# Whole loads of k, four small loads on another queue, two new ordering waits and one new rule of a planner

## The chip, the cores and the metric

The kernel runs on one NeuronCore of a Trainium2 chip. The metric is the device time of one execution in microseconds (us). Engines are named as the profile names them: PE (matmul) with PEld (its weight loads), DVE (VectorE), ACT (ScalarE), POOL (GpSimd), SP (SyncE, which here only issues DMAs). "SPq" and "ACTq" are DMA issues on SP and on ACT.

## The reference

Batch 4, 12 heads, 448 tokens, head size 64, so a model width of 768.

```python
def _attn_ref(q, k, v, g_q, g_k):
    q_n, k_n = (rmsnorm(q, g_q), rmsnorm(k, g_k))
    scores = scale * np.matmul(q_n, k_n.transpose(0, 1, 3, 2))
    scores = scores - np.max(scores, axis=-1, keepdims=True)
    attn = np.exp(scores)
    attn = attn / (np.sum(attn, axis=-1, keepdims=True) + 1e-09)
    return np.matmul(attn, v)
...
# then, per token or over tokens:
h = np.maximum(x @ w_in, 0.0); u, v = split(h)             # gated mixer
gated = u * (w_spatial over tokens of layernorm(v) + b);  x = gated @ w_out
u = x + (relu(x.T @ w_tok1) @ w_tok2).T                    # second mixer
out = u + relu(u @ w_ch1) @ w_ch2
```

g_q and g_k are vectors of 64 numbers, which reach the scores as one product.

## The kernel before

The 48 heads are worked in 24 pairs. For a pair, q and k (each 112 partitions x 4 chunks x 2 heads x 64) are loaded into one tile `raw`. ACT squares both halves into `sq` (for the very first k into a tile named `e`), DVE sums the squares into `ss`, POOL and ACT make the inverse root (`r0a`, `r0y`, `r0z` for q and `r8a`, `r8y`, `r8z` for k of the first pair; `ra`, `ry`, `rz` later), `raw` is scaled in place (DVE for the first pair, POOL later), PE transposes it into a PSUM tile `tp`, and a copy with the product `gg` of g_q and g_k gives k its gains. In the first 8 pairs the two transposed tiles are named `whole`, later `qt` and `kt`. PE then makes the scores `sc`, for one chunk of 112 tokens of both heads at a time: each head has 64 rows, so a score matmul fills half of the array's rows, and the two heads run beside each other. DVE takes the negated row maximum `nm`, ACT the exponential `e` with its sum. PE transposes `e` (`tp<-ident,e`), ACT or DVE copies it to `et`, and PE makes `av` from `et` and v: 64 output columns a head, half of the array's columns, again two heads beside each other. v lies in `v32` and its last 64 tokens in `vrest`, which holds zeros in its other half.

After six pairs (one batch entry) the first mixer's matmuls (`vps`, `ups`, `sps`, `xps`) are ready to run among the attention work of later pairs; the second mixer (`h1ps`, `u_ps`, `h2ps`, `o_ps`) follows. The weights arrive as 64-bit floats: `raw` pieces of them are turned into 32-bit numbers by ACT and DVE in tiles named `word` (for w_in's second half) and `wpart`.

Nothing of this is written in issue order by hand. `Plan` records every operation with an assumed cost, and `place` is a list scheduler, run forwards and backwards over the recorded operations, whose result is the order of each engine; all instructions are therefore issued at one line (L422). On PE `place` keeps half-array work together: when the next operation is of another kind than the one before (`parts` 1 for scores, 2 for `av`, 0 for the whole array) it looks for a waiting operation of the kind in hand that is nearly as urgent (`NEAR`). Each engine runs its instructions strictly in the order it was given. DMA completions are counted on 8 semaphores in rotation (named DMAHW0 to DMAHW7 in the order's rows), shared by SP's and ACT's DMAs: a ninth DMA waits until the one eight places earlier has landed.

The program opens (`start`) with 26 matmuls on zeros (`warm`), while the first two pairs are loaded.

Of the kernel before, what the change touches and what calls it, by code (L numbers as in the profile page):

```python
# [21 lines left out]
HI, LO = 0, 1  # L22
# [127 lines left out]
class Plan:  # L150
# [116 lines left out]
    def place(self, before, after, lag, weight, tiles=None):  # L267

        ops = self.ops
        left = [len(x) for x in before]  # L270
        ready = [0.0] * len(ops)
        engines = sorted({op.engine for op in ops})
        due = {e: [] for e in engines}
        waiting = {e: [] for e in engines}
        free_at = dict.fromkeys(engines, 0.0)
        start = [0.0] * len(ops)
        parts, port = 0, 0.0
        bank = {}
        if tiles is not None:
            opens, closes, users = tiles  # L280
            users = dict(users)
            free_banks = [(0.0, n) for n in range(Banks.ALL)]
            held = dict.fromkeys(Banks.OWN, 0)
            blocked = []
        for i, op in enumerate(ops):
            if not left[i]:
                heapq.heappush(due[op.engine], (0.0, i))
        placed = 0
        while placed < len(ops):
            t, e = min(  # L290
                (free_at[e] if waiting[e] else max(free_at[e], due[e][0][0]), e)
                for e in engines if waiting[e] or due[e])
            free_at[e] = t
            while due[e] and due[e][0][0] <= t:
                i = heapq.heappop(due[e])[1]
                heapq.heappush(waiting[e], (weight[i], i))
            i = heapq.heappop(waiting[e])[1]
            if e == "tensor" and ops[i].parts != parts:

                near = [x for x in waiting[e] if ops[x[1]].parts == parts and x[0] <= weight[i] + NEAR]  # L300
                if near:
                    x = min(near)
                    waiting[e].remove(x)
                    waiting[e].append((weight[i], i))
                    heapq.heapify(waiting[e])
                    i = x[1]
            other = SHARED.get(e)
            if ops[i].port and port <= t and other in due and free_at[other] <= t:

                free_at[other] = t  # L310
                while due[other] and due[other][0][0] <= t:
                    x = heapq.heappop(due[other])[1]
                    heapq.heappush(waiting[other], (weight[x], x))
                if waiting[other] and waiting[other][0][0] < weight[i] and ops[waiting[other][0][1]].port:
                    heapq.heappush(waiting[e], (weight[i], i))
                    e = other
                    i = heapq.heappop(waiting[e])[1]
            if ops[i].port:
                if port > t:
                    heapq.heappush(due[e], (port, i))  # L320
                    continue
                port = t + ops[i].cost
            if tiles is not None and i in opens:
                ks = opens[i]
                kind = ks[0].psum
                spare = len(free_banks) - sum(max(0, n - held[x]) for x, n in Banks.OWN.items() if x != kind)
                if spare < len(ks):
                    blocked.append(i)
                    continue
                free_banks.sort()  # L330
                at = free_banks[len(ks) - 1][0]
                if at > t:
                    heapq.heappush(due[e], (at, i))
                    continue
                for k in ks:
                    n = max(x for x in free_banks if x[0] <= t)
                    free_banks.remove(n)
                    bank[k] = n[1]
                held[kind] += len(ks)
            placed += 1  # L340
            start[i] = t
            end = t + ops[i].cost
            if e == "tensor":
                end += SWITCH * (ops[i].parts != parts)
                parts = ops[i].parts
            free_at[e] = end
            for s, hop in zip(after[i], lag[i]):
                ready[s] = max(ready[s], end + hop)
                left[s] -= 1
                if not left[s]:  # L350
                    heapq.heappush(due[ops[s].engine], (ready[s], s))
            if tiles is not None:
                for k in closes.get(i, ()):
                    users[k] -= 1
                    if not users[k]:
                        at = end + ops[i].late + TO["tensor"]
                        free_banks.append((at, bank[k]))
                        held[k.psum] -= 1
                        for x in blocked:
                            heapq.heappush(due["tensor"], (at, x))  # L360
                        blocked = []
        return start, max(free_at.values()), bank
# [107 lines left out]
def attention_moe_mixer(  # L470
# [7 lines left out]
    nc = tc.nc  # L478
# [55 lines left out]
    def wdram(w):  # L534
        return w.bitcast(U32)

    def convert(pool, tag, bufs, raw, rows, n, dst_hi, dst_lo, dims=None, at=None):

        if f64:
            r = raw.rearrange("p (n w) -> p n w", w=2)  # L540
            a = pool.tile([rows, n], U32, tag=tag, bufs=bufs, name="word") if at is None else at
            low, high = r[:, :, 0], r[:, :, 1]
            nc.scalar.activation(a.bitcast(F32), high.bitcast(F32), AF.Abs)
            nc.vector.tensor_scalar(a.bitcast(F32), a.bitcast(F32), least, most, ALU.max, ALU.min)
            nc.vector.tensor_scalar(a, a, 5, 2, ALU.logical_shift_left, ALU.logical_shift_right)
            nc.vector.scalar_tensor_tensor(a, high, 0xC0000000, a, ALU.bitwise_and, ALU.bitwise_or)
            nc.vector.scalar_tensor_tensor(a, low, 29, a, ALU.logical_shift_right, ALU.bitwise_or)
        else:
            a = raw
        a = a.bitcast(F32)  # L550
        if dst_hi is not None:
            v = a.rearrange("p (a b) -> p a b", a=dims[0]) if dims else a
            nc.scalar.activation(dst_hi, v, AF.Copy)
            nc.gpsimd.tensor_tensor(dst_lo, v, dst_hi.bitcast(F32), op=ALU.subtract)
        return a
# [43 lines left out]
    def mm_tile(name):  # L599
        return psum.tile([P, 512], "mm", name)  # L600

    def rsqrt(pool, src, n, w, mul, tag, bufs=2, on=None):

        on = on or nc.vector
# [3 lines left out]
        on.tensor_scalar(a[:n], src, mul, 1e-6, ALU.mult, ALU.add)  # L608
        nc.scalar.activation(y[:n], a[:n], AF.Ln)
        nc.scalar.activation(y[:n], y[:n], AF.Exp, scale=-0.5)  # L610
        on.tensor_tensor(z[:n], y[:n], y[:n], op=ALU.mult)
        on.tensor_tensor(z[:n], z[:n], a[:n], op=ALU.mult)
        on.tensor_scalar(z[:n], z[:n], -0.5, 1.5, ALU.mult, ALU.add)
# [7 lines left out]
    class Attention:  # L621
# [9 lines left out]
        def load(self, i):  # L631
# [4 lines left out]
            for r in range(2):  # L636
                nc.sync.dma_start(
                    out=t[:, 0, :, r], in_=q[b, 2 * j + r].rearrange("(c p) d -> p c d", p=T))
            on = nc.sync if i else nc.scalar
            on.dma_start(out=t[:, 1, :, 0], in_=k[b, 2 * j].rearrange("(c p) d -> p c d", p=T))  # L640

            src = k[b, 2 * j + 1]
            on.dma_start(out=t[:R, 1, 0, 1], in_=src[LAST:])
            on.dma_start(out=t[R:, 1, 0, 1], in_=src[:T - R])
            on.dma_start(
                out=t[:, 1, 1:, 1], in_=src[T - R:LAST].rearrange("(c p) d -> p c d", p=T))
            self.raw[i] = t
            if i == 2:
                self.third = t.tile
# [1 line left out]
        def load_v(self, i):  # L651
# [4 lines left out]
            rest = self.rests[i % VB]  # L656
            for r in range(2):
                src = v[b, 2 * j + r]
                nc.sync.dma_start(out=t[:, r], in_=src[:LAST].rearrange("(c p) d -> p c d", p=P))
                nc.sync.dma_start(out=rest[r * R:(r + 1) * R, r], in_=src[LAST:])  # L660
            self.v32[i] = t, rest

        def norms(self, i):
# [6 lines left out]
            for h in (slice(0, n // 2), slice(n // 2, n)):  # L670
# [2 lines left out]
                    sq = sq[:, :n // 2 * D].rearrange("p (n d) -> p n d", d=D)  # L673
                else:
                    sq = p.tile([T, n // 2, D], F32, tag="sq", bufs=1, name="sq")
                nc.scalar.activation(sq, raw[:, h], AF.Square)
                nc.vector.reduce_sum(ss[:T, h], sq, axis=AX.X)
                if i == 0:
# [155 lines left out]
        def start(self):  # L834
            self.load(0)
            g = self.p.tile([P, 2], F32, tag="g", bufs=1, name="g")
            for r in range(2):
                nc.sync.dma_start(out=g[r * D:(r + 1) * D, 0:1], in_=g_q.unsqueeze(1))
                nc.sync.dma_start(out=g[r * D:(r + 1) * D, 1:2], in_=g_k.unsqueeze(1))
            self.gg = self.p.tile([P, 1], F32, tag="gg", bufs=1, name="gg")  # L840
            nc.vector.tensor_tensor(self.gg, g[:, 0:1], g[:, 1:2], op=ALU.mult)
            nc.vector.tensor_scalar(self.gg, self.gg, float(D) ** -0.5, None, ALU.mult)
# [48 lines left out]
    ET, EB = 2 * C - 1, 5  # L891
    ON_DVE = (1, 1), (3, 1)
    SLOT = 8
    WARM = 26
    TWO = 99
    PREP0, LAG, SPAN = 1, 0.2, 5.8
    UO0, UO1 = 3, 11.5
# [4 lines left out]
    def prepare_v(mp):  # L902
# [5 lines left out]
        for j in range(KD):  # L908

            wait = [op for _, op in at.third.writers] if j > 1 else ()  # L910
            raw = weights(mp, "vn", 4, wdram(w_in)[j * P:(j + 1) * P, DU * W:], P, (DU,), wait)
            convert(mp, "vr", 2, raw, P, DU, wv[:, HI, j], wv[:, LO, j])
            yield
        for c in range(C):
            s = mp.tile([T, S], F32, tag="vn", bufs=4, name="stage")
# [570 lines left out]
```

## Time and profile before

| | |
|---|---|
| median of 3 runs | 891.25 us (890.48 to 892.96) |
| the profiled execution: its time | 892.5 us |
| its span (first to last instruction) | 890.7 us, 1.8 us less than its time |
| PE busy | 867.3 us, 97% of the span |
| DVE, ACT, POOL busy | 684.7, 538.3, 416.7 us |
| granted PE clock, mean | 0.996 of full speed |

A busy time is a sum over the whole span and over stages with different limits. The clock is given as a share of 2.4 GHz; 0.50 is 1.2 GHz.

### The profile page before, as it was taken

To read this page: it belongs to the slowest core of one execution; us is meant where nothing else is said; L and a number is where in the kernel's file an instruction comes from. 1 tells how busy PE (TensorE), PEld (TensorE's weight loads), DVE (VectorE), ACT (ScalarE), POOL (GpSimd) and SP (SyncE) were. 2 spreads that over 40 slices of the span, in tenths; PEclk is the share of its full clock that TensorE was granted. 3 is DMA by queue.
4 is the path that set the end of the run, shared out by engine and by line. 5 is a ranking of instruction groups with operands and counts; after the bars stand their busy time and mean duration, and the time that the engine had idled before them with its cause. 6 is when DMAs were issued, how large, how long until landed. Compare 5 with 4: busy or idle time off the path is not lost.

```text
span 890.7 us, 15921 instructions
## 1 busy us (share of the span) xinstructions
PE 867.3 (97%) x5186; PEld 721.6 (81%) x5186; DVE 684.7 (77%) x1333; ACT 538.3 (60%) x1292; POOL 416.7 (47%) x541
## 2 busy tenths in 40 slices
PE   7898999999999999999999999999999999999998
PEld 5444567787777787777789999999988899999998
DVE  4799897877877867976565466889888886998973
ACT  4999988777876777776543446546324554343331
POOL 3555654795676745665233214234323207524550
PEclk8999999999999999999999999999999999999999
DMA  6555645757535565335687559677564745661441
GB/s 152 154 133 156 193 126 162 203 175 229 162 105 159 151 203 160 90 123 166 211 267 250 178 179 319 194 242 231 157 160 133 230 125 155 213 182 54 142 151 63
DMA packets 149106, 152.30 MB, mean 171 GB/s; under 512 B 77856, under 2 KB 130656, under 8 KB 147488
## 3 DMA queue, kind: packets, MB, share of 16 engines
q1 hardware_dynamic: 148064, 151.06, 56.8%
q8 instruction: 41, 0.67, 0.3%
q14 instruction: 41, 0.34, 0.1%
q10 hardware_dynamic: 960, 0.23, 0.1%
HBM read 112.44 MB, written 38.80 MB: 170 GB/s over the span
## 4 chain that ended last, share of the span: by engine, by line
PE 77%; ACT 9%; DVE 8%; DMA 3%; issue 2%; SPq 0%; POOL 0%; ACTq 0%; DVEq 0%
PE o_ps L422 15%; PE h2ps L422 15%; PE tp L422 8%; PE xps L422 6%; PE ups L422 6%; PE av L422 6%; PE vps L422 5%; PE sc L422 5%; PE sps L422 4%; ACT e L422 4%; PE h1ps L422 3%; PE u_ps L422 3%; ACT et L422 2%; DVE op L422 1%; DVE w L422 1%
## 5 line engine op out<-in xcount | busy, mean ns | idle before, releaser
L422 PE MATMUL h2ps<-op,w 128*128 128x448 f32 x756 | 155.8, 367 | 2.4 <-DVE c L422 2.3
L422 PE MATMUL o_ps<-w,op 128*128 128x384 f32 x882 | 153.6, 334 | 1.2 <-DVE u L422 1.2
L422 PEld LDWEIGHTS o_ps<-w,op 128*128 128x128 f32 x882 | 152.8, 188 | 1.8 <-issue 1.8
L422 PEld LDWEIGHTS h2ps<-op,w 128*128 128x128 f32 x756 | 141.1, 188 | 15.7 <-DVE c L422 4.4
L422 ACT ACTIVATE e<-sc,nm 112x448 f32<-112x448 f32 x192 | 122.5, 653 | 25.3 <-DVE nm L422 25.1
L422 DVE TENSOR_REDUCE nm<-sc 112x1 f32<-112x448 f32 x192 | 109.5, 615 | 17.3 <-PE sc L422 17.0
L422 POOL TENSOR_TENSOR src<-src 128x384 f32<-128x384 f32 x48 | 62.7, 1314 | 77.6 <-DMA src<-c_d 40.6
L422 PEld LDWEIGHTS tp<-ident,e 112*128 112x128 f32 x672 | 71.8, 141 | 32.9 <-ACT et L422 9.3
L422 POOL TENSOR_SCALAR e<-e,sums 112x448 f32<-112x448 f32 x112 | 75.3, 690 | 40.9 <-ACT sq L422 9.7
L422 PE MATMUL tp<-ident,e 112*128 112x112 f32 x672 | 88.7, 262 | 4.6 <-ACT et L422 2.4
L422 ACT ACTIVATE op<-c 128x768 fp32r<-128x768 f32 x49 | 41.5, 847 | 84.6 <-PE o_ps L422 81.2
L422 ACT ACTIVATE et<-tp 128x448 f32<-128x448 f32 x144 | 71.3, 530 | 15.3 <-PE tp L422 14.4
L422 DVE SCALAR_TENSOR_TENSOR word<-raw,word 128x256 uint32<-128x256 uint32 (+2 forms) x132 | 72.2, 553 | 1.4
L422 POOL TENSOR_TENSOR u<-u,o 128x384 f32<-128x384 f32 x28 | 40.2, 1453 | 66.5 <-ACT o L422 35.8
L422 DVE TENSOR_SCALAR word<-word 128x256 f32<-128x256 f32 (+5 forms) x132 | 59.6, 458 | 15.0 <-ACT word L422 14.2
L422 PE MATMUL ups<-xp,wu 128*128 128x448 f32 x288 | 69.1, 376 | 0.0
L422 DVE TENSOR_TENSOR op<-c,op 128x768 fp32r<-128x768 f32 x49 | 57.4, 1172 | 10.3 <-ACT op L422 10.3
L422 PE MATMUL xps<-wo,g 128*128 128x256 f32 x432 | 60.5, 289 | 0.0
L422 PE MATMUL vps<-wv,xp 128*128 128x512 f32 x216 | 59.7, 409 | 0.0
L422 PE MATMUL av<-et,v 128*64 128x448 f32 x288 | 59.6, 548 | 0.0
L422 PEld LDWEIGHTS xps<-wo,g 128*128 128x128 f32 x432 | 54.7, 190 | 5.8 <-issue 2.3
L422 DVE TENSOR_TENSOR c<-c,h2ps 128x448 f32<-128x448 f32 x84 | 50.0, 616 | 11.0 <-PE h2ps L422 10.3
(141 smaller groups left out, 1661.9 us busy)
## 6 DMA issues: line engine op xcount, KB each, us to landing
src<-c_d SPq DMA_DIRECT2D x132, 192.0 KB, 3.1
wu<-wu_d SPq DMA_DIRECT2D x16, 768.0 KB, 4.8
wo<-wo_d SPq DMA_DIRECT2D x12, 1024.0 KB, 5.4
raw<-in_moe_w_ch_dram SPq DMA_DIRECT2D x36, 256.0 KB, 3.5
raw<-in_moe_w_ch_dram SPq DMA_DIRECT2D x24, 384.0 KB, 3.7
raw<-in_q_dram SPq DMA_DIRECT2D x48, 112.0 KB, 2.9
u<-u_d SPq DMA_DIRECT2D x28, 192.0 KB, 3.9
out_dram<-u SPq DMA_DIRECT2D x28, 192.0 KB, 2.0
```

Of the source, the lines that this page charges most:

```text
L422: getattr(getattr(self.nc, op.engine), fn)(*args, **kwargs)
```

## The change

Six edits, in one version:

- k of the second head of a pair is loaded in token order by one DMA, where it was rolled by 64 tokens and came in three. The roll is made up for by v: the second head's `vrest` now takes the first 64 tokens and not the last. A pair has 2 DMAs for k in place of 4, and the same bytes.
- The four DMAs of g_q and g_k are issued from ACT, not from SP.
- The first two `word` tiles of the weight w_in wait for the copy that writes the first pair's k (`wait=behind`).
- The first Square of pair 1 waits for the two Exp operations of pair 0's inverse roots (`powers[:2]`).
- Where PE's next operation is of the whole array and half-array work was in hand, `place` may now take waiting half-array work of either kind, not of the same kind alone.
- 18 matmuls on zeros, not 26.

```diff
@@ place
                 near = [x for x in waiting[e] if ops[x[1]].parts == parts and x[0] <= weight[i] + NEAR]
+                if not near and parts and not ops[i].parts:
+                    near = [x for x in waiting[e] if ops[x[1]].parts and x[0] <= weight[i] + NEAR]
...
@@ convert
+            a.tile.after = list(a.tile.after) + list(wait)
...
@@ load
-            on.dma_start(out=t[:, 1, :, 0], in_=k[b, 2 * j].rearrange("(c p) d -> p c d", p=T))
-
-            src = k[b, 2 * j + 1]
-            on.dma_start(out=t[:R, 1, 0, 1], in_=src[LAST:])
-            on.dma_start(out=t[R:, 1, 0, 1], in_=src[:T - R])
-            on.dma_start(
-                out=t[:, 1, 1:, 1], in_=src[T - R:LAST].rearrange("(c p) d -> p c d", p=T))
+            for r in range(2):
+                on.dma_start(
+                    out=t[:, 1, :, r], in_=k[b, 2 * j + r].rearrange("(c p) d -> p c d", p=T))
...
@@ load_v
-                nc.sync.dma_start(out=t[:, r], in_=src[:LAST].rearrange("(c p) d -> p c d", p=P))
-                nc.sync.dma_start(out=rest[r * R:(r + 1) * R, r], in_=src[LAST:])
+
+                most, least = (src[:LAST], src[LAST:]) if r == 0 else (src[R:], src[:R])
+                nc.sync.dma_start(out=t[:, r], in_=most.rearrange("(c p) d -> p c d", p=P))
+                nc.sync.dma_start(out=rest[r * R:(r + 1) * R, r], in_=least)
...
@@ norms
+                    if i == 1:
+
+                        sq.tile.after = list(sq.tile.after) + powers[:2]
...
@@ start
-                nc.sync.dma_start(out=g[r * D:(r + 1) * D, 0:1], in_=g_q.unsqueeze(1))
-                nc.sync.dma_start(out=g[r * D:(r + 1) * D, 1:2], in_=g_k.unsqueeze(1))
+                nc.scalar.dma_start(out=g[r * D:(r + 1) * D, 0:1], in_=g_q.unsqueeze(1))
+                nc.scalar.dma_start(out=g[r * D:(r + 1) * D, 1:2], in_=g_k.unsqueeze(1))
...
-    WARM = 26
+    WARM = 18
...
@@ prepare_v
-            convert(mp, "vr", 2, raw, P, DU, wv[:, HI, j], wv[:, LO, j])
+
+            behind = [] if wait else [op for _, op in at.kt[0].tile.writers]
+            convert(mp, "vr", 2, raw, P, DU, wv[:, HI, j], wv[:, LO, j], wait=behind)
```

The planner then makes new orders for all engines. At three places they are shown here.

The first place is ACT from its first DMA to its first exponential (`e,sums<-sc,nm`). What each instruction waits for stands in brackets; DMAHW is the semaphore of a DMA. Before:

```order
L422 DMA raw<-in_k_dram 48x64 [waits DMAHW0_49]
L422 ACTIVATE sq<-raw 112x512 [waits DMAHW1_49]
L422 ACTIVATE e<-raw 112x512 [waits DMAHW4_49,DMAHW6_49,DMAHW2_49,DMAHW0_49]
...
L422 ACTIVATE ry<-ra 112x16 [waits Pool_49]
L422 ACTIVATE word<-raw 128x512 [waits DMAHW0_49]
L422 ACTIVATE whole<-tp,gg 128x448 [waits DVE_49,PE_49]
L422 ACTIVATE ry<-ry 112x16 [waits Activation_49]
L422 ACTIVATE word<-raw 128x512 [waits DMAHW1_49]
L422 ACTIVATE e,sums<-sc,nm 112x448 [waits DVE_49] x4
```

And now:

```order
L424 DMA g<-in_g_q_dram 64x1 [waits DMAHW1_49]
L424 DMA g<-in_g_k_dram 64x1 [waits DMAHW3_49]
L424 ACTIVATE sq<-raw 112x512
L424 ACTIVATE e<-raw 112x512 [waits DMAHW4_49,DMAHW2_49]
...
L424 ACTIVATE whole<-tp,gg 128x448 [waits PE_49]
L424 ACTIVATE ry<-ra 112x16 [waits Pool_49]
L424 ACTIVATE word<-raw 128x512 [waits DMAHW4_49]
L424 ACTIVATE ry<-ry 112x16 [waits Activation_49]
L424 ACTIVATE word<-raw 128x512 [waits DMAHW5_49]
L424 ACTIVATE wpart<-raw 128x256 [waits DMAHW2_49]
L424 ACTIVATE e,sums<-sc,nm 112x448 [waits DVE_49] x4
```

The copy of the first k (`whole<-tp,gg`) moved ahead of both `word` conversions, and a `wpart` conversion moved ahead of the exponentials. The first Square (`sq`) now stands behind four DMA issues, the last of which waits for DMAHW3; that semaphore is held by pair 1's first q, the fourth DMA of the program.

The second place is DVE at the same time, up to the first maxima (`nm`). Before:

```order
L422 TENSOR_REDUCE ss<-sq 112x8 [waits Activation_49]
L422 TENSOR_TENSOR gg<-g 128x1 [waits DMAHW6_49,DMAHW7_49,DMAHW5_49,DMAHW4_49]
L422 TENSOR_REDUCE ss<-sq 112x8 [waits Activation_49]
L422 TENSOR_TENSOR raw<-raw,r0y 112x512 [waits DMAHW1_49,DMAHW0_49,Pool_49]
L422 TENSOR_TENSOR raw<-raw,r8y 112x512 [waits DMAHW2_49,DMAHW0_49,Pool_49]
```

And now:

```order
L424 TENSOR_TENSOR gg<-g 128x1 [waits DMAHW3_49,DMAHW6_49,DMAHW1_49,DMAHW0_49]
L424 TENSOR_SCALAR gg<-gg 128x1 [waits DVE_49]
L424 TENSOR_REDUCE ss<-sq 112x8 [waits Activation_49]
L424 TENSOR_TENSOR raw<-raw,r0y 112x512 [waits Pool_49]
L424 TENSOR_TENSOR raw<-raw,r8y 112x512 [waits DMAHW4_49,DMAHW2_49,Pool_49]
L424 TENSOR_REDUCE ss<-sq 112x8 [waits Activation_49]
```

One of the two sums for pair 1 (`ss<-sq`) moved behind the scaling of pair 0; the other still stands ahead of it.

The third place is PE at one of the later pairs, in the stage where the first mixer's `vps` runs among attention. Before:

```order
L422 MATMUL sc<-kt,qt 112x448 x12
L422 MATMUL tp<-ident,raw 128x112 x8
L422 MATMUL av<-et,v_2794 64x448 x6
L422 MATMUL av<-et,vrest 64x448 x2
L422 MATMUL vps<-wv,xp 128x512 x9
```

And now, at the same pair:

```order
L424 MATMUL sc<-kt,qt 112x448 x12
L424 MATMUL av<-et,v_2846 64x448 x6
L424 MATMUL tp<-ident,raw 128x112
L424 MATMUL vps<-wv,xp 128x512 x5
L424 MATMUL av<-et,vrest 64x448 x2
L424 MATMUL sc<-kt,qt 112x448 x6
L424 MATMUL vps<-wv,xp 128x512
```

Here `av` stands right behind a group of scores, and its last two matmuls right ahead of another, but the `av` group is cut in two. Counted over the whole order of PE, the steps from whole-array to half-array work or back fall from 156 to 134, the steps from scores to `av` or back rise from 9 to 35, and all steps together go from 165 to 169. Up to the first `vps` they go from 60 (none between the two halves) to 64 (8 between them); from there on they are 105 in both.

## Rows read from the trace of the kernel before

**Rows 1.** Four stretches: busy us of each engine, granted clock, DMA share, GB/s.

```profile
core 0: us, PE busy (x) PEld busy (x) DVE busy (x) ACT busy (x) POOL busy (x), PEclk, DMA share, GB/s
13.00:15.10 2.10, 0.00 (x0) 0.00 (x0) 0.48 (x2) 1.21 (x3) 0.00 (x0) 0.65 1.08 308
15.10:20.00 4.90, 4.87 (x12) 1.53 (x12) 3.38 (x6) 2.96 (x9) 3.40 (x6) 0.50 0.67 176
20.00:100.00 80.00, 72.94 (x452) 38.19 (x451) 70.97 (x153) 78.12 (x221) 43.73 (x70) 1.00 0.57 157
100.00:880.00 780.00, 772.85 (x4628) 666.12 (x4627) 603.53 (x1163) 451.58 (x1052) 366.29 (x446) 1.00 0.58 174
```

**Rows 2.** The chain that ended last, first 20 us: start, length, what.

```profile
1.70 3.95 DMA raw<-in_q_dram
...
5.67 0.32 SPq L422
...
7.85 0.59 SPq L422
...
8.49 5.38 DMA raw<-in_moe_w_in_dram
```

**Rows 3.** Timeline, first 20 us: start, length, engine, operation, [idle before <-releaser].

```profile
1.50 8.59 PE L422 MATMUL warm<-vrest 128*128 128x128 f32 x52 [1.50 <-POOL vrest L422]
...
3.84 0.63 ACT L422 ACTIVATE sq<-raw 112x512 f32<-112x512 f32 x1 [1.82 <-DMA raw<-in_q_dram]
4.50 0.69 DVE L422 TENSOR_REDUCE ss<-sq 112x8 f32<-112x512 f32 x1 [4.50 <-ACT sq L422]
...
6.49 0.63 ACT L422 ACTIVATE e<-raw 112x512 f32<-112x512 f32 x1 [2.02 <-DMA raw<-in_k_dram]
...
8.40 0.21 ACT L422 ACTIVATE r8y<-r8y 112x8 f32<-112x8 f32 x1
...
10.26 0.16 DVE L422 TENSOR_TENSOR gg<-g 128x1 f32<-128x1 f32 x1 [1.79 <-DMA g<-in_g_k_dram]
...
10.93 0.68 DVE L422 TENSOR_TENSOR raw<-raw,r0y 112x512 f32<-112x512 f32 x1
...
11.53 0.69 DVE L422 TENSOR_TENSOR raw<-raw,r8y 112x512 f32<-112x512 f32 x1
...
11.71 1.16 PE L422 MATMUL tp<-ident,raw 112*128 112x112 f32 x8 [1.62 <-issue]
...
13.89 0.66 ACT L422 ACTIVATE word<-raw 128x512 f32<-128x512 f32 x1 [1.96 <-DMA raw<-in_moe_w_in_dram]
14.45 0.62 ACT L422 ACTIVATE whole<-tp,gg 128x448 f32<-128x448 f32 x1
14.58 0.89 DVE L422 TENSOR_SCALAR word<-word 128x512 f32<-128x512 f32 x2 [1.63 <-ACT word L422]
...
15.13 5.15 PE L422 MATMUL sc<-whole 64*112 64x448 f32 x12 [2.25 <-ACT whole L422]
...
17.00 1.16 DVE L422 TENSOR_REDUCE nm<-sc 112x1 f32<-112x448 f32 x2 [0.80 <-PE sc L422]
17.66 0.64 ACT L422 ACTIVATE e<-sc,nm 112x448 f32<-112x448 f32 x1 [1.71 <-DVE nm L422]
```

**Rows 4.** PE's timeline where half-array groups meet each other.

```profile
173.61 0.47 PE L422 MATMUL sps<-ws,vn 128*128 128x448 f32 x1
174.02 2.48 PE L422 MATMUL av<-et,v 128*64 128x448 f32 x12
...
177.18 1.06 PE L422 MATMUL sc<-kt,qt 64*112 64x448 f32 x8
```

**Rows 5.** PE's timeline where whole-array work follows av.

```profile
249.50 2.48 PE L422 MATMUL av<-et,v 128*64 128x448 f32 x12
...
252.65 1.67 PE L422 MATMUL vps<-wv,xr 128*128 128x512 f32 x6
```

**Rows 6.** The page's costliest group: count, busy us, mean ns.

```profile
L422 PE MATMUL h2ps<-op,w 128*128 128x448 f32 x756 | 155.8, 367 | 2.4 <-DVE c L422 2.3
```

More of the change, by code (lines that the diff above doesn't have):

```diff
@@ L535, in wdram, with convert @@
         return w.bitcast(U32)
-    def convert(pool, tag, bufs, raw, rows, n, dst_hi, dst_lo, dims=None, at=None):
+    def convert(pool, tag, bufs, raw, rows, n, dst_hi, dst_lo, dims=None, at=None, wait=()):
         if f64:
@@ L600, in mm_tile @@
         return psum.tile([P, 512], "mm", name)
+    powers = []
     def rsqrt(pool, src, n, w, mul, tag, bufs=2, on=None):
@@ L610, in rsqrt @@
         nc.scalar.activation(y[:n], y[:n], AF.Exp, scale=-0.5)
+        powers.append(nc.ops[-1])
         on.tensor_tensor(z[:n], y[:n], y[:n], op=ALU.mult)
```

## The prediction

> **What bounds the kernel now.** I read the stretches first: the question is which engine is full where. From 100 us to 880 us PE is busy 772.85 of 780 us, at a granted clock of 1.00; from 20 to 100 us ACT is busy 78.12 of 80 us and PE only 72.94 [rows 1]. So there are three stages: an opening of about 20 us in which nothing is full, a stage that ACT bounds, and a long one that PE bounds. The work of the last two doesn't change in amount, so what the opening loses or wins should come out at the end almost whole, as long as the new order keeps ACT and then PE as full as before.
>
> Then the chain of waits over the opening, to see what ends last there. It runs through DMAs and issues: pair 1's first q, issued at 1.70 us, takes 3.95 us to land; SP goes on at 5.67 us with the last piece of pair 1's k, which needed that semaphore, then issues the four small loads (the last at 7.85 us, 0.59 us each), and only at 8.49 us the weight w_in, whose 5.38 us end at 13.87 us [rows 2]. In the timeline ACT's `word` waits for this until 13.89 us, and the first pair's k copy (`whole`) stands behind it at 14.45 us, although its transposes ended at 12.87 us (11.71 + 1.16); the scores start at 15.13 us, the first maximum at 17.00 and the first exponential at 17.66 us [rows 3]. The clock had fallen meanwhile: 0.65 on average over 13.0 to 15.1 us, 0.50 over 15.1 to 20.0 us, that is 1.2 GHz, with PE idle over the 2.25 us ahead of the scores [rows 1, 3]. A second, shorter line of waits ends earlier: `gg` waits for the last small load until 10.26 us, and the scaling of q and k (10.93 and 11.53 us) stands behind it on DVE [rows 3].
>
> **The change, the opening.** Which line is late next? I follow the new order with the old durations.
>
> The weights no longer stand ahead of k's copy. That alone frees the copy from 14.45 us to the end of the transposes, 12.87 us: 1.6 us.
>
> The small loads land earlier, but they aren't free on ACT. The first two wait for little. The fourth uses the semaphore of pair 1's first q, which landed at 5.65 us [rows 2]; I take the same again, since about the same bytes are queued ahead of it. So ACT issues its last DMA at about 5.7 us, needs 0.59 us for it, and the first Square, which ran at 3.84 us, starts at 6.3 us. The second Square (`e<-raw`) follows 0.54 to 0.63 us later, at 6.87 us; it ran at 6.49 us, because k landed late [rows 3]. By this the earlier landing of k (two whole loads instead of four pieces) is worth nothing: ACT is not there to use it. What is behind the waiting DMA on ACT is the whole norm of pair 0, and DVE, POOL and PE wait for that.
>
> From the second Square to the end of the root's last Exp (8.40 us) it took 1.91 us. Add 0.1 us, since DVE now has the sum of q (0.69 us) just ahead of that of k: Exp at 8.88 us. Pair 1's first Square, now behind it, starts at 9.1 us; DVE's sum follows 0.66 us later (3.84 to 4.50), at 9.75 us; the scaling of q after a step of 0.60 us (10.93 to 11.53), at 10.35 us, that of k at 10.95 us. `gg` costs nothing: the last small load, issued at 5.7 us, needs about what it did before (from 7.85 us until DVE went on at 10.26 us, so 2.4 us) and is there at 8.1 us, or 9 us if the weights slow it, and DVE is free of it well before 9.75 us. From the scaling of k to the end of the transposes it took 1.34 us (11.53 to 12.87): 12.3 us. ACT's copy then starts at once and the scores 0.68 us later (14.45 to 15.13), at 12.97 us in place of 15.13: **2.16 us** earlier.
>
> From the scores to the first maximum it took 1.87 us at 1.2 GHz, and 0.66 us on to the exponential. If the clock is low again from the start, the exponential comes at 15.5 us: 2.16 us won. PE's pauses say it will fall again: zeros end near 8 us now (16 of 52 records fewer of 8.59 us, at their mean or a little less) [rows 3], and to 12.97 us there are only the short transposes. If it falls somewhat later than the scores start, the first pair of them is quicker, by up to 0.9 us. But DVE has two `word` operations (0.89 us) ahead of the first maximum, and ACT two `word` and one `wpart` ahead of the exponential, which must have landed: w_in now goes out behind k, at about 5.5 us rather than 8.49, so even with 6 us it is there at 11.5 us, and `wpart`, five issues of some 0.6 us later and past a wait for the zeros, out at about 9 us and, with w_in's 5.38 us, there at 14.4 us. That leaves no more than 0.5 us of the 0.9. I take 0.25 us more: **2.4 us** in all, with bounds of 1.5 us (`wpart` or q a microsecond late) and 3.0 us.
>
> **The change, the rest.** SP issues 46 DMAs fewer in the other 23 pairs, 0.3 to 0.6 us each by the two in [rows 2]. None of PE's idle time after the opening ends on a DMA of k, and PE is idle only 7.15 us from 100 to 880 us [rows 1]; I cost it at 0, with a gain of 1 us as the bound. Eight fewer matmuls on zeros: 0, they end before the transposes are ready either way. v's other end: same bytes, 0.
>
> The rule of the planner: a step between whole and half array costs about 0.1 us. One `sps` matmul alone between scores and `av` takes 0.41 us (173.61 to 174.02) [rows 4], where one of the same shape takes 0.206 us in a long run (155.8 / 756) [rows 6]; that is 0.2 us for two steps. Does joining scores with `av` save any? `av` takes 3.16 us from start to the scores that follow it (174.02 to 177.18) [rows 4] and 3.15 us to whole-array work (249.50 to 252.65) [rows 5]. So going from one half to the other costs what going to the whole array costs, and what counts are all steps: 165 before, 169 now, and 105 in both where PE is the bound. The four more lie where ACT is the bound: 0 us, 0.4 us as the bound. The Trainium skill says the same against this edit: TensorEngine Tiling (Array Packing), "Tiling Modes", Key Properties, has it that a change of tiling mode, not only of tile, drains TensorE, and the two kinds are two modes. By that page the sum stays.
>
> If only steps to and from the whole array counted, 22 fewer would give 2.2 us more.
>
> The sum: 892.5 - 2.4 = 890.1 us for an execution like the profiled one. That one lies 1.25 us above the median of the runs, so **888.8 us** against the median of 891.25 us.
>
> **The rivals.**
> *The clock stays up (chance 0.15).* At 2.4 GHz the twelve score records would need about half of their 5.15 us. The first exponential is held by DVE's and ACT's weight work, but the second and third chunk's are not, and ACT is idle less: some 1.4 us more, 3.8 us in all, 887.4 us. For it: the pause right ahead of the scores shrinks from 2.25 us to about 0.7 us. Against it: the pause after the zeros grows from 1.6 us to 2 or 3 us.
> *Nearly nothing is won (0.19).* k's 96 KB that came late are now ahead of pair 1's first q. If that lands 2 us later, at 7.7 us, ACT's first Square does too, and everything after it: 0.2 us won, 891.0 us, no change. It decides linearly, microsecond for microsecond.
> *Half to half is free (0.06).* 22 steps at 0.1 us: 886.6 us. [rows 4, 5] speak against it.
> *Slower: the joined `av` starves ACT (0.12).* Where scores and `av` now touch, an `av` group of 3.16 us may run ahead of scores that ACT waits for, and up to the first `vps` ACT has no time to lose. There are 8 such places there and none before. If ACT runs dry for 0.65 us at each, 5.2 us are lost and 2.4 won: 894.0 us. The point where it decides is 0.3 us at each. Against it: the scores of one chunk are in hand while the next are made. The same name covers a new order that leaves PE idle later.
>
> **How the numbers follow.** The forecast itself has a chance of 0.48, with a range of its own of 888.0 to 889.8 us. 0.3%, here 2.7 us, is what a measurement of this kernel can tell from no change: the limits are 888.6 and 893.9 us. The forecast lies just inside, so I split it, 0.22 faster and 0.26 same. Faster: 0.22 + 0.15 + 0.06 = 0.43. Same: 0.26 + 0.19 = 0.45. Slower: 0.12. The range of 8 in 10 reaches from the free half steps with a good opening, 886.0 us, to 892.0 us, which leaves out most of the slower case.
>
> **What the profile would show.** Right: ACT's first Square at about 6.3 us behind its own DMA issues, k's copy at 12.3 us with no `word` ahead of it, the scores near 13 us, the first exponential between 14.7 and 15.7 us, and from 20 to 100 us ACT as full as before. Wrong in the opening: the Square before 5 us or after 7 us, or a clock of 1.00 over the first scores. Wrong in the rest: PE or ACT idle for `nm` or `e` right after an `av` group before 100 us, or PE idle for clearly more or less than 7 us from 100 to 880 us.

## The result and the profile after

The changed kernel takes **900.39 us** (median of 6 runs, 897.83 to 901.51) against 891.26 us for the kernel before in the same runs: a ratio of 1.0094, with a 95% interval of 1.0077 to 1.0110. (The ratios on record are worked out over all runs and need not equal the quotient of two medians, which is 1.0102 here.) It is slower by 9 us; 888.8 us was predicted. The profiled execution took 901.39 us with a span of 899.3 us.

The windows of the changed kernel, in the same stretches as [rows 1] and around three places more (columns: window, length, then busy time and count of PE, PEld, DVE, ACT, POOL; granted clock, DMA share, GB/s):

```profile
7.00:10.70 3.70, 0.65 (x6) 0.46 (x5) 0.40 (x1) 1.35 (x5) 1.75 (x10) 1.00 0.89 265
13.00:15.10 2.10, 1.38 (x8) 1.03 (x9) 1.03 (x2) 0.94 (x3) 0.21 (x1) 0.50 0.01 1
15.10:20.00 4.90, 4.90 (x17) 1.74 (x17) 3.52 (x7) 3.82 (x11) 3.20 (x6) 0.59 0.67 166
20.00:100.00 80.00, 74.96 (x460) 38.31 (x460) 71.47 (x158) 78.73 (x224) 46.32 (x72) 1.00 0.57 154
100.00:880.00 780.00, 766.92 (x4564) 656.82 (x4563) 595.97 (x1153) 444.46 (x1044) 364.85 (x445) 1.00 0.58 174
...
258.00:262.00 4.00, 4.00 (x17) 3.62 (x17) 1.86 (x6) 1.99 (x4) 3.47 (x6) 0.57 0.00 0
449.00:453.00 4.00, 4.00 (x14) 1.10 (x10) 1.44 (x4) 0.44 (x1) 0.00 (x0) 0.57 0.78 246
```

ACT is as full from 20 to 100 us as before (78.73 of 80 us). The loss comes later: from 100 to 880 us PE is idle for 13.1 us, 7.15 before [rows 1]. Two of those 4 us stretches have a granted clock of 0.57: 3.4 us of each at 0.50 (1.2 GHz), the rest at 1.00, which by an estimate from these shares costs 1.7 us each without showing as idle time. In this execution 6 us more of idle time and 3.4 us of clock, less the 0.3 us that the opening won, are the 9 us.

The timeline of the changed kernel at the three places (start, duration, engine, operation; in brackets the idle time before it and what ended it; SPq and ACTq are DMA issues):

```profile
4.26 1.54 SPq L424 DMA_DIRECT2D raw<-in_moe_w_in_dram  x2
4.94 0.47 ACTq L424 DMA_DIRECT2D g<-in_g_k_dram  x1
5.46 0.63 ACT L424 ACTIVATE sq<-raw 112x512 f32<-112x512 f32 x1 [3.44 <-DMA g<-in_g_k_dram]
10.75 0.16 DVE L424 TENSOR_TENSOR gg<-g 128x1 f32<-128x1 f32 x1 [3.35 <-DMA vrest<-in_v_dram]
12.21 0.69 DVE L424 TENSOR_TENSOR raw<-raw,r8y 112x512 f32<-112x512 f32 x1
14.16 0.63 ACT L424 ACTIVATE whole<-tp,gg 128x448 f32<-128x448 f32 x1 [1.80 <-PE tp L424]
14.84 4.39 PE L424 MATMUL sc<-whole 64*112 64x448 f32 x10 [0.72 <-ACT whole L424]
17.37 0.63 ACT L424 ACTIVATE e<-sc,nm 112x448 f32<-112x448 f32 x1 [0.93 <-DVE nm L424]
...
244.10 0.60 DVE L424 TENSOR_TENSOR lrz<-lry 128x1 f32<-128x1 f32 x1
...
250.04 2.60 POOL L424 TENSOR_SCALAR e<-e,sums 112x448 f32<-112x448 f32 x4 [2.14 <-PE av L424]
251.12 2.78 DVE L424 TENSOR_TENSOR lrz<-lry 128x1 f32<-128x1 f32 x1
252.60 1.29 POOL L424 TENSOR_TENSOR vn<-vr,vn 128x512 fp32r<-128x512 f32 x1
253.82 0.61 DVE L424 TENSOR_REDUCE nm<-sc 112x1 f32<-112x448 f32 x1
254.47 0.63 ACT L424 ACTIVATE e<-sc,nm 112x448 f32<-112x448 f32 x1 [2.79 <-DVE nm L424]
255.95 1.03 PE L424 MATMUL tp<-ident,e 112*128 112x112 f32 x7 [1.65 <-ACT e L424]
...
447.75 0.70 ACT L424 ACTIVATE xo<-xps 128x256 f32<-128x256 f32 x2 [4.69 <-DMA x_d<-xo]
448.18 3.81 PE L424 MATMUL av<-et,v 128*64 128x448 f32 x12 [3.04 <-ACT xo L424]
```

- **Opening.** The scores start at 14.84 us and the first exponential at 17.37, each 0.3 us earlier than in [rows 3]; 2.16 and 2.4 us were predicted. DVE stands at `gg` until 10.75 us. The bracket names a `vrest` load, but what `gg` reads is the last g, issued at 4.94 us: it lands 5.6 us after its issue and DVE goes on 5.8 us after it, with both first pieces of w_in (128x1024 words each) issued on SP from 4.26 us and the DMA engines busy 0.89 of the time from 7 to 10.7 us.
- **First stall.** At 251.12 us DVE takes 2.78 us over 128 numbers; the same operation of the pass before, at 244.10 us, took 0.60, and half of the sixteen in this kernel take 0.16 or less. It ends when POOL's `vn` ends (252.60 + 1.29 = 253.89). The planner does have a rule that keeps DVE operations with two operands in SBUF apart from POOL's, but only where the second operand has more than one column (`len(sbuf) > 1 and free(sbuf[1].shape) > 1`), so to the planner this operation collides with nothing. `nm`, ACT's `e` and PE's `tp` follow, with 1.65 us of idle PE, and from 258 us the clock is at 0.50.
- **Second stall.** `xo` has two places; ACT waits 4.69 us for the store of an earlier one before it can empty PE's bank. PE stands still for 3.04 us, and then the clock falls again (`av`, 12 records, takes 3.81 us).

### The profile page after: what moved, and what is told of

Its sections match the earlier page's. It is cut to its first block, busy times and chain, and to the rows that moved or that the text cites. A ratio compares the mean times of both kernels' runs of the same rounds, so it can differ in the third digit from the quotient of the medians.

```text
span 899.3 us, 15791 instructions
## 1 busy us (share of the span) xinstructions
PE 870.8 (97%) x5170; PEld 720.0 (80%) x5170; DVE 681.7 (76%) x1333; ACT 534.9 (59%) x1292; POOL 417.4 (46%) x541
## 4 chain that ended last, share of the span: by engine, by line
PE 74%; DVE 10%; ACT 7%; DMA 4%; issue 2%; POOL 1%; SPq 0%; ACTq 0%; DVEq 0%; POOLq 0%
PE o_ps L424 15%; PE h2ps L424 12%; PE tp L424 8%; PE av L424 6%; PE ups L424 6%; PE xps L424 6%; PE sc L424 6%; PE vps L424 4%; PE sps L424 4%; PE u_ps L424 3%; PE h1ps L424 3%; ACT e L424 3%; DVE word L424 2%; DVE c L424 2%; DMA wu_d<-wpart 1%
## 5 line engine op out<-in xcount | busy, mean ns | idle before, releaser
L424 POOL TENSOR_TENSOR src<-src 128x384 f32<-128x384 f32 x48 | 66.2, 1390 | 80.0 <-DMA src<-c_d 37.7
L424 POOL TENSOR_SCALAR e<-e,sums 112x448 f32<-112x448 f32 x112 | 72.7, 666 | 43.2 <-DVE sums L424 30.2
L424 DVE SCALAR_TENSOR_TENSOR word<-raw,word 128x256 uint32<-128x256 uint32 (+2 forms) x132 | 70.4, 539 | 1.3
L424 DVE TENSOR_SCALAR word<-word 128x256 uint32<-128x256 uint32 (+5 forms) x132 | 58.6, 454 | 15.5 <-ACT word L424 14.7
L424 PE MATMUL av<-et,v 128*64 128x448 f32 x288 | 62.1, 560 | 3.0 <-ACT xo L424 3.0
L424 PE MATMUL xps<-wo,g 128*128 128x256 f32 x432 | 62.5, 290 | 0.1
L424 PEld LDWEIGHTS ups<-xp,wu 128*128 128x128 f32 x288 | 53.1, 191 | 6.2 <-ACT word L424 0.7
```

Source lines behind the costliest of these rows:

```text
L424: getattr(getattr(self.nc, op.engine), fn)(*args, **kwargs)
```

## The experiments

The expectations name Theory 1 (the join rule makes the later order worse, the rest is worth its small gain), Theory 2 (any edit makes the planner draw a new order, and the loss is a few collisions that its costs don't know) and Theory 3 (moving the opening's loads is what costs). Each ratio is against the kernel before in the same runs, with its 95% interval; medians of different groups stand against different runs of that kernel (891.26 to 891.81 us), so a microsecond between two of them is not clear of noise.

**1. Which edits lose the time.** Four versions, parts of the change:

```diff
 no_join:    the changed kernel without
-                if not near and parts and not ops[i].parts:
-                    near = [x for x in waiting[e] if ops[x[1]].parts and x[0] <= weight[i] + NEAR]
 join_only:  the kernel before, with these two lines
 waits_only: the kernel before, with the two ordering waits (behind, powers[:2])
 k_only:     the kernel before, with whole loads of k and v's other end
```

> The changed kernel without the planner's join rule; all else of the change stays. Theory 1 (the join rule makes the order after the opening worse, the rest of the change is worth its small gain in the opening): 890 to 891 us, and no fall of the clock after 20 us. Theory 2 (any edit makes the planner draw a new order, and the losses are collisions that its costs don't contain, so they come and go with each order): some time between 888 and 900 us, with stalls at other places than in the changed kernel. Theory 3 (the opening's data movement, whole loads of k and small loads from ACT, costs the time): still 899 to 901 us.

> The kernel before with the join rule alone. Theory 1: 899 to 902 us, with PE stalls of 1.5 to 3 us between 240 and 450 us, each with a fall of the clock behind it. Theory 2: another order again, 888 to 900 us, stalls not at the same places as in the changed kernel. Theory 3: 891 us as before.

> The kernel before with the two ordering waits alone (first word tiles behind the first k copy, pair 1's first Square behind the first roots). The small loads stay on SP, so w_in goes out as late as before. Opening: k's copy no longer waits for w_in, first scores near 13.6 us against 15.1, 1.5 us won there. Theory 1: 889 to 891 us in all. Theory 2: the opening's gain, and after it an order that is as likely to lose as to win several us: 888 to 900 us.

> The kernel before with whole loads of k (and v's other end) alone. 46 fewer DMA issues on SP. Opening: little, first k lands some 1.5 us earlier, but gg and w_in still end last; w_in goes out about 1 us earlier. Theory 1: 890 to 891 us. Theory 2: 887 to 900 us with another order. Theory 3: 895 us or more.

| version | median, us (lowest to highest) | ratio |
|---|---|---|
| no_join | 890.67 (888.29 to 895.25) | 0.9996 [0.9978, 1.0014] |
| join_only | 895.04 (893.88 to 896.08) | 1.0042 [1.0027, 1.0056] |
| waits_only | 892.69 (890.88 to 893.67) | 1.0007 [0.9995, 1.0018] |
| k_only | 890.60 (889.11 to 895.98) | 1.0004 [0.9986, 1.0021] |

So Theory 3 falls: with all of the opening's edits and no join rule the kernel is not slower. The join rule carries the loss, but not by one amount: 3.2 us alone (895.04 against 891.81 us for the kernel before in these runs), 9.7 us with the rest (900.39 against 890.67). Alone it has neither of the changed kernel's two stalls: from 100 to 880 us PE's longest wait is 1.2 us, and the clock falls nowhere behind the opening. What shows in its place is that ACT is less full than before where ACT is the bound (30 to 100 us, first join_only, then the kernel before):

```profile
30.00:100.00 70.00, 63.05 (x391) 32.74 (x392) 63.73 (x130) 66.47 (x187) 44.35 (x69) 1.00 0.56 155
30.00:100.00 70.00, 64.92 (x404) 34.02 (x405) 61.29 (x134) 68.57 (x193) 42.05 (x64) 1.00 0.59 163
```

Of ACT's waits from 20 to 100 us in join_only the longest, 1.7 us, is for DVE's work on a weight (`wpart`), not for `av`.

The timeline of no_join's opening comes near to what the prediction had followed:

```profile
5.14 0.47 ACTq L422 DMA_DIRECT2D g<-in_g_k_dram  x1
6.11 0.49 SPq L422 DMA_DIRECT2D raw<-in_moe_w_in_dram  x1
...
5.66 0.63 ACT L422 ACTIVATE sq<-raw 112x512 f32<-112x512 f32 x1 [3.65 <-DMA g<-in_g_k_dram]
7.77 0.16 DVE L422 TENSOR_TENSOR gg<-g 128x1 f32<-128x1 f32 x1 [0.17 <-DMA g<-in_g_k_dram]
11.51 0.63 ACT L422 ACTIVATE whole<-tp,gg 128x448 f32<-128x448 f32 x1 [1.23 <-PE tp L422]
12.19 1.76 PE L422 MATMUL sc<-whole 64*112 64x448 f32 x8 [0.72 <-ACT whole L422]
14.79 0.62 ACT L422 ACTIVATE e<-sc,nm 112x448 f32<-112x448 f32 x1
```

Here w_in goes out at 6.11 us, behind v and behind the last g, and `gg` runs at 7.77 us: the scores come 2.9 us earlier than before. The join rule, a rule about PE, had thus moved SP's loads in the changed kernel.

The table shows something else as well: an earlier opening isn't yet a shorter kernel. The first exponential, at 17.66 us before [rows 3], comes at 15.57 us in waits_only, at 14.79 in no_join and at 14.32 in k_only, where the whole loads of k alone let SP issue the four g from 3.83 us and w_in from 6.36 us, in place of 8.49:

```profile
8.12 0.16 DVE L422 TENSOR_TENSOR gg<-g 128x1 f32<-128x1 f32 x1 [1.21 <-DMA g<-in_g_k_dram]
14.32 0.63 ACT L422 ACTIVATE e<-sc,nm 112x448 f32<-112x448 f32 x1 [0.58 <-DVE nm L422]
```

That is 2.1, 2.9 and 3.3 us won, but the medians move by +0.9, -1.1 and -1.2 us, and no interval of the three leaves out that nothing changed (waits_only was to be at 889 to 891 us if its gain were kept). In the profiled executions of no_join and k_only, both at a mean clock of 1.000, the gain is there: their spans are 887.6 and 888.2 us, against 890.7. Other executions of the two took up to 895.25 and 895.98 us; they left no trace, so where the gain goes in them stays open.

**2. Where the rule acts.** Its condition is limited to work written in the first 100 us or so of the program, or to later work, or to a quarter of its reach:

```diff
 join_early:
-                if not near and parts and not ops[i].parts:
+                if not near and parts and not ops[i].parts and i < 1000:
 join_late:
+                if not near and parts and not ops[i].parts and i >= 1000:
 near_half:
-... x[0] <= weight[i] + NEAR]
+... x[0] <= weight[i] + NEAR // 4]
```

> The changed kernel, but the join rule holds only for work that the program writes in about its first 100 us. Theory 1a (joining scores and av starves ACT early, as the rival in the prediction has it): nearly all the loss is here, 898 to 900 us. Theory 1b (joining hurts where PE is the bound): as without the rule, about 890.7 us. Theory 2 (a rule that the planner meets anywhere draws a whole new order, and what the time is depends on which collisions that order has): no place decides, 891 to 900 us. In each, the opening is late if gg lands behind w_in, since this order has both w_in pieces ahead of v on SP as the changed kernel does: first scores near 14.8 us and not 12.2.

> The changed kernel, but the join rule holds only for work that the program writes after about its first 100 us. Theory 1a: no loss, about 890.7 us. Theory 1b: nearly all the loss, 898 to 900 us. Theory 2: 891 to 900 us, and the orders differ before 100 us too although the rule isn't met there; both w_in pieces stand ahead of v on SP here as well, so the first scores should come near 14.8 us and not 12.2.

> The changed kernel, but a work item is pulled forward by the join rule only from a quarter as far. Theory 1 (the farther the rule reaches, the more it pulls out of turn): between the kernel without the rule and the changed one, 892 to 896 us. Theory 2: anything from 890 to 900 us, without regard to how far the rule reaches. Here one w_in piece stands ahead of v on SP and one behind, so gg should land between 7.8 and 10.7 us.

| version | median, us (lowest to highest) | ratio |
|---|---|---|
| join_early | 894.36 (890.38 to 896.03) | 1.0028 [1.0012, 1.0043] |
| join_late | 889.96 (888.66 to 893.25) | 0.9984 [0.9970, 0.9998] |
| near_half | 893.15 (890.99 to 897.00) | 1.0022 [1.0004, 1.0039] |

No place holds the 9.7 us: against no_join the early rule costs 3.7 us, the late one nothing. Of the 3.7 us the opening has 2.4: join_early's `gg` runs at 10.68 us and its first exponential at 17.14; the other 1.3 us are not placed. near_half lies in the range of both theories and decides nothing between them. In join_early ACT doesn't starve (78.86 of 80 us from 20 to 100 us). And join_late, which doesn't apply the rule before 100 us at all, has w_in ahead of v on SP all the same and the latest `gg` of all (DVE's timeline):

```profile
11.22 0.16 DVE L424 TENSOR_TENSOR gg<-g 128x1 f32<-128x1 f32 x1 [3.56 <-DMA v<-in_v_dram]
```

The planner goes over the whole program forwards and backwards and keeps the shortest plan; a rule met late redraws the beginning. That the order is redrawn is the first half of Theory 2 (its range, 891 us and more, was a little too high for join_late). Whether the loss is then a few collisions, the next group tests with the order held still.

**3. The stalls taken away, in the joined order.** These keep the changed kernel's order on every engine (late_v_first that of join_late), except for what the diff moves:

```diff
 after_xo4:     four places for xo, unknown to the planner
-                xo = mp.tile([P, NX], F32, tag="xo", bufs=2, name="xo")
+                xo = mp.tile([P, NX], F32, tag="xo", bufs=2, real=4, name="xo")
 after_xo4_lr:  the same, and on DVE (name <- operands)
-lrz<-lry  nm<-sc  lrz<-lrz,lra  nm<-sc x3
+nm<-sc x4  lrz<-lry  lrz<-lrz,lra
 after_v_first: the changed kernel, and on SP
-w_in x2  v x2  vrest x2
+v x2  w_in  vrest x2  w_in
 after_all:     all three
 late_v_first:  join_late, and on SP the first w_in behind v, the second behind vrest
```

> The changed kernel with its order kept instruction for instruction on every engine; only the tile xo has four places instead of two, so that ACT's copy at 447.75 us need not wait 4.69 us for a store. If the loss is made of stalls of this kind and of the clock that falls behind them: PE's 3.0 us idle and about half of the 3.4 us at the half clock go, 4.7 us, so 895 to 896.5 us. If the loss is in the joined order itself (more steps, less overlap everywhere): 899 to 900 us. If what waits there is held by something else too: 898 us, with a new idle time at the same place.

> The changed kernel with four places for xo, its order kept, except that on DVE the two small operations lrz<-lry and lrz<-lrz,lra of one pass (those that took 2.78 us beside GpSimd at 251.12 us in the changed kernel) go behind the four nm reductions, not among them. If the small operation holds DVE while GpSimd's e and vn run, and nm, ACT's e, PE's tp and the clock follow: PE's 1.66 us idle and half of the 3.4 us at the half clock go, 3.4 us less than the kernel with four places for xo alone (897.27 us), so 893.5 to 894.5 us. If DVE is held by something else there: 897 us, and the first nm is as late as before.

> The changed kernel with its order kept on every engine, except that SP issues v's two loads ahead of the two w_in loads (the second w_in behind the two small v loads). If it is w_in that makes the last g load land at 10.7 us: gg at 7.8 to 8.2 us, first scores at 12.2 us instead of 14.84, and, if the rest of the order keeps it, 2 to 2.6 us less than the changed kernel, 897.8 to 898.4 us. If gg is late for another reason, or the stage that ACT bounds eats the gain: 900 us. The loss of some 10 us would not be explained by the opening in either case.

> The changed kernel's order with all three: four places for xo, the two small operations behind nm, and v ahead of w_in on SP; nothing else is moved, and the join rule's order stays. If the loss against the kernel without the rule is the sum of a few such stalls: 897.3 - 3.4 - 2.4 = 891.5 us, 890.5 to 892.5 us. If the joined order costs by itself (more steps, ACT starved all along): 895 us or more.

> The kernel with the join rule for the later work only (889.96 us), its order kept, except that SP issues v ahead of w_in. Its gg came at 11.22 us and its first exponential at 17.84 us, the latest of all. If the opening's gain is kept to the end: 2.5 to 3.2 us less, about 887 us, faster than both kernels by over 0.3%. If a later stall eats it: 889 to 890 us.

| version | median, us (lowest to highest) | ratio |
|---|---|---|
| after_xo4 | 897.27 (893.74 to 898.62) | 1.0053 [1.0038, 1.0068] |
| after_xo4_lr | 894.69 (893.74 to 896.13) | 1.0040 [1.0025, 1.0055] |
| after_v_first | 896.44 (893.05 to 898.33) | 1.0042 [1.0013, 1.0071] |
| after_all | 890.59 (888.10 to 893.13) | 0.9984 [0.9968, 0.9999] |
| late_v_first | 887.28 (886.36 to 888.88) | 0.9960 [0.9946, 0.9974] |

after_xo4, PE's timeline and two windows where the second stall was:

```profile
444.55 2.48 PE L424 MATMUL av<-et,v 128*64 128x448 f32 x12
...
445.00:449.00 4.00, 4.00 (x22) 1.89 (x19) 1.00 (x3) 1.00 (x3) 0.00 (x0) 1.00 0.91 283
449.00:453.00 4.00, 4.00 (x19) 3.31 (x18) 0.98 (x3) 0.44 (x2) 0.29 (x1) 1.00 0.88 289
```

The wait and the fall of the clock are both gone, worth 3.0 + 1.7 us at the place; 3.1 us of it arrives at the end (4 to 5.4 were expected). Part is given back: PE waits 1.1 us for ACT's `h` later, which it doesn't in the changed kernel.

after_xo4_lr, timelines of DVE, POOL and PE and one window at the first stall:

```profile
252.39 2.21 DVE L429 TENSOR_REDUCE nm<-sc 112x1 f32<-112x448 f32 x4
253.90 1.29 POOL L429 TENSOR_TENSOR vn<-vr,vn 128x512 fp32r<-128x512 f32 x1
254.52 0.68 DVE L429 TENSOR_TENSOR lrz<-lry 128x1 f32<-128x1 f32 x1
255.41 0.83 PE L429 MATMUL tp<-ident,e 112*128 112x112 f32 x7
...
258.00:262.00 4.00, 4.00 (x25) 3.64 (x24) 2.49 (x8) 2.40 (x5) 2.81 (x4) 1.00 0.06 9
```

`nm` is ready when PE gets there, PE doesn't wait, and the clock stays at 1.00: 2.6 us less than after_xo4 by the medians, 3.4 expected. By the runs alone this step isn't clear of noise (four runs, and the intervals of the two ratios overlap); it is the trace of the place that shows it.

after_v_first, timelines of DVE, PE and ACT, and one window:

```profile
7.43 0.16 DVE L427 TENSOR_TENSOR gg<-g 128x1 f32<-128x1 f32 x1
12.07 1.76 PE L427 MATMUL sc<-whole 64*112 64x448 f32 x8 [0.72 <-ACT whole L427]
15.00 0.62 ACT L427 ACTIVATE e<-sc,nm 112x448 f32<-112x448 f32 x1
445.04 2.48 PE L427 MATMUL av<-et,v 128*64 128x448 f32 x12 [1.68 <-ACT xo L427]
...
448.00:452.00 4.00, 4.00 (x19) 3.15 (x18) 1.29 (x4) 0.98 (x2) 0.29 (x1) 1.00 0.94 288
```

w_in's first load behind v's two, and its second behind `vrest` too, bring `gg` from 10.75 to 7.43 us and the scores from 14.84 to 12.07. The gain of 3.95 us (2 to 2.6 were expected) is more than the opening's, 2.8 us at the scores and 2.4 at the first exponential: the wait at `xo` is 1.68 us here and the clock doesn't fall after it.

after_all, one window:

```profile
100.00:880.00 780.00, 770.59 (x4609) 664.00 (x4610) 596.98 (x1154) 445.79 (x1040) 363.01 (x439) 1.00 0.58 174
```

With the three stalls gone and the joined order otherwise as it was, the kernel is at 890.59 us, where no_join is (890.67). The three steps, 3.1 + 2.6 + 4.1 us, are the whole loss (9.7 us against no_join). The last is again 1.3 us more than the scores' 2.8; which later wait gave that isn't settled. So Theory 1 falls in the form that joining costs by itself: beyond these three stalls no cost shows, with about 1.5 us of uncertainty on either time. The comparison isn't quite even, since no_join kept its own short waits and none was taken away by hand: from 100 to 880 us PE is idle for 9.4 us in after_all and for 7.6 in no_join.

late_v_first was expected at about 887 us and is at 887.28, 0.4% faster than the kernel before: it has the opening's gain and none of the stalls. Whether its late joining adds to that, or only drew a good order, no run tells.

## Why the prediction was wrong, by its steps

- **The opening's working held, in another order than the changed kernel's.** For no_join each step came within 0.9 us of it: first Square 6.3 us predicted and 5.66 measured, `gg`'s load 8.1 and 7.77, scores 12.97 and 12.19, first exponential 14.7 to 15.7 and 14.79. One reading in it is loose: 8.40 us is the start of the last Exp, not its end [rows 3]; the 9.1 us that follow allow for its 0.21 us.
- **The step that failed in the opening** is "`gg` costs nothing", with the load "there at 8.1 us, or 9 us if the weights slow it". The prediction had the last g out at 5.7 us on ACT and w_in "at about 5.5 us" on SP, so it had them side by side, and gave the load 2.4 us as before [rows 3], or 3.3 us. In the changed kernel w_in goes out from 4.26 us and the last g at 4.94 us, and `gg` runs 5.8 us after that; in no_join, with w_in a microsecond behind the g, it runs 2.6 us after it (5.14 to 7.77). The wait was seen, its size was not. This took 2.1 of the 2.4 us. How long a small load needs beside a megabyte stood in no row of the kernel before, where the g loads go ahead of w_in, so 9 us was too near a bound.
- **The premise that failed** is that a gain of the opening "should come out at the end almost whole, as long as the new order keeps ACT and then PE as full as before". With the order held still a gain arrives: from join_late to late_v_first the first exponential comes 3.4 us earlier (17.84 and 14.43 us) and the median is 2.7 us lower. With a new order it need not: no_join's 2.9 us are 1.1 us at the end, not clear of noise. The condition was written down, but the sum gave it no price, so even without the join rule 888.8 us was not reached.
- **The step that failed in the rest** is the join rule's "0 us, 0.4 us as the bound". Counting steps between whole and half array was right as far as it went: after_all has the joined order's steps and is level with no_join, so neither a cost of the steps nor a saving from half to half shows (0.1 us between them, with about 1.5 us of uncertainty on each). The TensorEngine Tiling (Array Packing) page of the Trainium skill, "Tiling Modes", had spoken against such a saving, and nothing here speaks for it. But the rule's price isn't in its steps. It is in the new order of all engines, which put one small DVE operation beside POOL's work and PE's `av` behind a store: 8.1 us of PE's time (1.65 + 3.04 us idle, twice 1.7 us of clock), of which taking both away gives back 5.7 at the end.
- **That the clock "will fall again"** was right for the changed kernel: 0.50 over 13.0 to 15.1 us. In no_join, whose PE is idle less, it stays at 1.00 in the profiled execution; that was the rival with 0.15.
- **The rivals.** "Slower" came true by its sign, but its mechanism, `av` starving ACT before 100 us, didn't: in the changed kernel ACT is as full as before, and the rule limited to that stage keeps it so. In join_only alone ACT is 2.0 us less busy from 20 to 100 us (76.12 against 78.12), and its longest wait there is not for `av`. Only the rival's last sentence, a new order that leaves PE idle later, names what happened; it had no price and so nothing in the range. "Nearly nothing is won" came near the opening's 0.3 us by luck: its cause was a late q of pair 1, but ACT's first Square runs at 5.46 us, earlier than forecast.
- **What would show it wrong** did: PE idle for clearly more than 7 us from 100 to 880 us.

## What to carry to other kernels

In a kernel whose order a planner draws, an edit to the planner's rules must be costed as a new order of every engine's queue, not by what the rule counts: read where loads have changed places and which short waits now end on PE, and keep a loss of 1% in the range. What such an edit wins in one place has not been won until the redrawn rest has kept it. To find where such a loss sits, freeze the order and take away one stall at a time; here three edits, none of them to the rule, brought all of it back. Small loads that the first chain needs belong ahead of the big ones in time, on whatever queue: here a load on ACT's queue was late because of a megabyte on SP's.

## What the runs showed of the hardware

- A DVE operation with two operands of 128x1 took 2.78 us while POOL worked through the rest of its four `e` operations and then `vn`, and ended with the last of them; moved back, it took 0.68 us and ended with POOL's `vn` again (254.52 + 0.68 against 253.90 + 1.29). The Trainium skill has this in SBUF — State Buffer, "SBUF: two separate sides": a DVE instruction with two SBUF inputs and a GpSimd instruction that reads SBUF lock each other out, and the one that comes first keeps the ports for its whole length. The trace agrees, and adds that DVE didn't get in between one POOL instruction and the next.
- The clock is not decided by the length of one pause. PE idle for 1.65 us ahead of `tp` at 255.95 us was followed by 3.4 us at 0.50; idle for 1.68 us ahead of `av` at 445.04 us in after_v_first, by 1.00 throughout.
- Executions of one kernel differ in their mean clock, and their times go with it only in part. The two of after_v_first at 1.000 took 893.05 and 893.18 us, the four at 0.994 to 0.996 took 895.19 to 898.33 us; but of k_only's, one at 1.000 took 893.21 us and one at 0.997 took 890.09 us.
